# Weight sums by adding transfers, and four more pairs taken back from chunk two's stores

## The chip, the cores and the metric

The kernel runs on one core of a Trainium2 chip. The metric is the device time of one execution in microseconds, the median of the runs. The engines are TensorE (PE in the profile), VectorE (DVE), ScalarE (ACT), GpSimd (POOL) and SyncE (SP, which here issues nearly all transfers).

## What is computed

```python
def _attn_ref(u, v, z):                       # u, v: 4 x 3008 x 256, z: 4 x 3008 x 64
    scores = (1.0 / S) * np.matmul(z, z.transpose(0, 2, 1))
    attn = np.maximum(scores, 0.0) ** 2
    return (u * np.matmul(attn, v)).astype(np.float32)

def _moe_ref(x, w_gate, w_val, w_out):        # x: 12032 x 256, weights 256 x 1536 and 1536 x 256, float64
    gate = 1.0 / (1.0 + np.exp(-(x @ w_gate)))
    return (gate * (x @ w_val) @ w_out).astype(np.float32)
```

The result of the first is the input x of the second. The scores are symmetric: the block of keys i and queries j is the transpose of the block of keys j and queries i. The weights come as 64-bit floats, which the kernel turns into 32-bit ones itself.

## The kernel before, in words

**Tiling.** Each of the four batches has six chunks of 512 queries (c = 0 to 5, the last 448) and twelve pairs of 128 keys (k = 0 to 11). A step g is one (batch, chunk, pair), 288 in all: step 0 to 11 is chunk 0 of batch 0 ("chunk one"), 12 to 23 "chunk two", 24 to 35 "chunk three". Every product is done with operands split in a high part and a rest (ah and al, vh and vl, and so on), so that three matmuls stand for one. In a step TensorE does the scores of a later pair (`pe_scores`, 4 matmuls into the bank sc), the product of this step's pair with v (`pe_pv`, 12, into acc), and from step 24 on the gate and value products of the chunk two before (`pe_gv`, 12, into gv) and its output product (`pe_out`, 6).

**Order.** It is written out by hand (`manual_schedule`): the loop over the steps names, call by call, what each engine's queue gets, and each engine works its queue strictly in order. `post_scores(nxt)` puts Relu and Square on ScalarE (L379, L380, result r), ah on ScalarE or VectorE (L388, L390) and al on VectorE (L391). `gate` puts the sigmoid on ScalarE and a product on VectorE (L549), after which the gv bank is free again. For chunks one and two nxt is two steps ahead, from chunk three on one step.

**Taking blocks back.** `turn` writes r to DRAM turned, block by block, where a later chunk can use the block instead of computing its scores (`kept`, `load_back`). For the first two chunks of batch 0 VectorE has no time to turn. There `stored` pairs (k = 6 to 9) are written as they are (L453), from single buffers that are otherwise weight tiles: chunk two's alternate between the two buffers oh1 and ol1. `arrange` (L420) then copies them within DRAM, 16 issues for each 512x512 block, so that chunks four and five can read them as 32x32 blocks (`late`, `load_back`) and VectorE turns these when they are back (`turn_late`, L483). Steps 12 to 27 issue four such copies each. In chunks four and five `pair` takes the pairs in the order 4, 5, 0 to 3 and then 6 on, so that the late ones do not come first.

**Weights.** Ten jobs (`w_jobs`) turn 64-bit words into 32-bit floats in steps 6 to 35. A job loads raw words (`load_w`, L163, on SP), takes their absolute value on ScalarE, shifts, puts the sign back, and forms the low words' share on VectorE (`low_words`, or piece by piece in `low_by_piece`), adds it (L207, or L217 for a piece), and then splits the sum into a high part (ScalarE, L227) and a rest (VectorE, L230). `plan` says in which step each part is called, before (`w_before`) or after (`w_after`) the step's `post_scores`. The scratch for a piece's share is the single buffer zraw for jobs four to seven.

**SP's queue.** It carries all loads of u, v, z and weights, the stores, the rearranging copies and the loads of blocks. POOL's queue carries no transfer.

Of the kernel before, what the change touches and what calls it, by code (L numbers as in the profile page):

```python
# [8 lines left out]
F32 = mybir.dt.float32  # L9
# [3 lines left out]
U32 = mybir.dt.uint32  # L13
AF = mybir.ActivationFunctionType
ALU = mybir.AluOpType
# [13 lines left out]
def kernel(  # L29
# [19 lines left out]
    nc = tc.nc  # L49
    P = 128  # L50
# [52 lines left out]

    def pair(b, c, k):

        if b == 0 and c in (3, 4) and k < 6:
            return (k + 4) % 6
        if not halved(b, c) or k <= 2 * c:
            return k
        return k + 1 if k < NPAIR - 1 else 2 * c + 1  # L110

    def half(b, c, k):
        return halved(b, c) and k == NPAIR - 1


    def back(b, c, k):
        return kept(b, pair(b, c, k) // 2, c) or late(b, c, k)

    def stored(b, c, k):
        return b == 0 and c < 2 and 6 <= k < 10  # L120

    def late(b, c, k):

        return b == 0 and c in (3, 4) and pair(b, c, k) < 4


    w_tiles = {}
# [37 lines left out]
    class Narrow:  # L165
# [38 lines left out]
                )  # L204

        def add(self):
            nc.vector.tensor_tensor(self.fa, self.fa, self.b.bitcast(F32), op=ALU.add)  # L207

        def low_by_piece(self):
            for r, t in zip(self.part, self.raws):  # L210
# [48 lines left out]
    def prep_z_high(b, s):  # L259
        zt = zt_t[b, s]  # L260
        zP = zp.tile([P, CH], F32R, tag="zP", name="zP")
        zQ = zp.tile([P, CH], F32R, tag="zQ", name="zQ")
        if (b, s) == (0, 1):
            nc.vector.tensor_copy(zP[0:64], zt[0:64])
        else:
            nc.scalar.activation(zP[0:64], zt[0:64], AF.Copy)
        if b > 0:
            nc.scalar.activation(zQ[64:128], zt[64:128], AF.Copy)
        z_t[b, s] = zP, zQ

    def prep_z_low(b, s):
        zt, (zP, zQ) = zt_t.pop((b, s)), z_t[b, s]
        if (b, s) == (0, 0):
            nc.vector.tensor_copy(zQ[64:128], zt[64:128])
        if twice(b, s):
            nc.vector.tensor_tensor(zP[64:128], zt[64:128], f32(zQ[64:128]), op=ALU.subtract)
        nc.vector.tensor_tensor(zQ[0:64], zt[0:64], f32(zP[0:64]), op=ALU.subtract)
        if not twice(b, s):
            nc.sync.dma_start(f32(zQ[64:128]), f32(zP[0:64]))
            nc.sync.dma_start(f32(zP[64:128]), f32(zQ[0:64]))  # L280
# [84 lines left out]
    def post_scores(b, c, k):  # L365
        n = chunk(c)
        sc = sc_t.pop((b, c, k), None)
        if back(b, c, k):
            r = r_t.pop((b, c, k))
        else:  # L370
            if half(b, c, k):
                r = r_t.pop((b, c, k))
            elif stored(b, c, k):
                tag = ("gh4", "gl4", "gh2", "gl2")[k - 6] if c == 0 else ("oh1", "ol1")[k % 2]
                r = one.tile([P, 2, CH], F32, tag=tag, name="r")
            else:
                r = two.tile([P, 2, CH], F32, tag="r", name="r")
            q0 = CH // 2 if half(b, c, k) else 0
            nc.scalar.activation(by_halves(r[:, :, q0:n]), products(sc[:, :, 0 : n - q0]), AF.Relu, scale=scale)  # L379
            nc.scalar.activation(r[:, :, q0:n], r[:, :, q0:n], AF.Square)  # L380
        if early(b, c) and k % 3 == 2:
            ah = one.tile([P, 2, CH], F32R, tag="gh5", name="ah")
            al = one.tile([P, 2, CH], F32R, tag="gl5", name="al")
        else:
            ah = two.tile([P, 2, CH], F32R, tag="ah", name="ah")
            al = two.tile([P, 2, CH], F32R, tag="al", name="al")
        if back(b, c, k) or (b, c) == (0, 2) or (b, c) == (0, 1) and k % 3 or (b, c) == (0, 0) and k in (7, 10):
            nc.scalar.activation(ah[:, :, 0:n], r[:, :, 0:n], AF.Copy)  # L388
        else:
            nc.vector.tensor_copy(ah[:, :, 0:n], r[:, :, 0:n])  # L390
        nc.vector.tensor_tensor(al[:, :, 0:n], r[:, :, 0:n], f32(ah[:, :, 0:n]), op=ALU.subtract)  # L391
        a_t[b, c, k] = ah, al
        r_t[b, c, k] = r
# [21 lines left out]
    def arrange(c, e, n):  # L415

        if (c, e) not in blocks_t:
            blocks_t[c, e] = dram.tile([CH // 32, 32, CH // 32, 32], F32, name=f"blocks_{c}_{e}")
        src = stored_t[c, e][:, 32 * n : 32 * n + 32].rearrange("(G p) q -> p G q", p=32)
        nc.sync.dma_start(blocks_t[c, e][n], src)  # L420
# [39 lines left out]
    def load_back(b, c, k):  # L460
        n = chunk(c)
        if late(b, c, k):
            i = pair(b, c, k)
            t = two.tile([P, 2, CH], F32, tag="osb", name="blocks")
            src = blocks_t[i // 2, c][(i % 2) * 8 : (i % 2) * 8 + 8]
            nc.sync.dma_start(t, src.rearrange("(j a) p G q -> (a p) j (G q)", j=2))
            r_t[b, c, k] = t
            return
        r = two.tile([P, 2, CH], F32, tag="r", name="r")
        if half(b, c, k):  # L470
            nc.sync.dma_start(r[:, :, 0 : CH // 2], half_t[b, c].rearrange("(j p) q -> p j q", p=P))
            r_t[b, c, k] = r
            return
        i = pair(b, c, k)
        src = turned_t[b, i // 2, c][(i % 2) * 256 : (i % 2) * 256 + 256, 0:n]
        nc.sync.dma_start(r[:, :, 0:n], src.rearrange("(j p) q -> p j q", p=P))
        r_t[b, c, k] = r

    def turn_late(b, c, k):
        t = r_t.pop((b, c, k))  # L480
        r = two.tile([P, 2, CH], F32, tag="r", name="r")
        for j in range(2):
            nc.vector.transpose(out=r[:, j], in_=t[:, j])  # L483
        r_t[b, c, k] = r

    def pe_pv(b, c, k):
# [128 lines left out]
    w_load.update({10: [(2, 0)], 11: [(2, 1)]})  # L615
    w_load.update({12 + n: [(3, n)] for n in range(4)})
    w_load.update({17 + n: [(4, n)] for n in range(4)})
    w_load.update({24: [(5, 0), (5, 1)], 25: [(6, n) for n in range(4)], 27: [(7, n) for n in range(4)]})
    w_load.update({26: [(8, 0)], 29: [(9, 0)]})
    w_scratch = [("xh", "xl"), ("oh2", "ol2")] * 2  # L620
    w_scratch += [("oh2", "zraw"), ("ol2", "zraw")] * 2 + [("zraw", "ol2"), ("zraw", "vraw")]
    w_before, w_after, w_raw, w_run = {}, {}, {}, {}

    def plan(i, start):

        def at(when, g, *ops):
            when.setdefault(g, []).extend((i, op) for op in ops)
        at(w_after, start, ("abs",))
        if i < 4:
            at(w_before, start + 1, ("shift",), ("sign", 0))  # L630
            at(w_before, start + 2, ("sign", 1), ("power",))
            at(w_before, start + 3, ("low_words",))
            at(w_before, start + 4, ("add",))
            at(w_before, start + 5, ("high_part",))
            at(w_after, start + 5, ("low_part",))
        elif i < 8:
            at(w_before, start + 1, ("shift",), ("sign", 0), ("sign", 1))
            at(w_before, start + 2, ("low_by_piece",))
            at(w_before, start + 3, ("high_part",))
            at(w_after, start + 3, ("low_part",))  # L640
        else:
            at(w_before, start + 1, ("shift",), ("sign", 0))
            at(w_before if i == 8 else w_after, start + (2 if i == 8 else 1), ("low_by_piece",))
            at(w_after if i == 8 else w_before, start + 2, ("high_part",))
            at(w_after, start + 2, ("low_part",))

    for i, start in enumerate([6, 10, 14, 18, 23, 25, 27, 29, 31, 33]):
# [13 lines left out]
    with tc.manual_schedule():  # L661
# [50 lines left out]
        for g, (b, c, k) in enumerate(steps):  # L712
# [18 lines left out]
            if C == 0:  # L731
                if k + 2 < NPAIR:
                    prep_v_low(0, k + 2)
                if k + 5 < NPAIR:
                    load_v(0, k + 5)
                if k in (2, 3, 5):
                    prep_z_low(0, {2: 3, 3: 4, 5: 5}[k])
                if k in (0, 2, 4):
                    turn_z(0, k // 2 + 3)
            weights(w_before.get(g, ()))  # L740
# [1 line left out]
                post_scores(*nxt)  # L742
            if C == 0 and k + 3 < NPAIR:
                prep_v_high(0, k + 3)
            if C == 0 and k in (1, 2, 4):
                prep_z_high(0, {1: 3, 2: 4, 4: 5}[k])
            for n, s in enumerate(steps[g + 2 : g + 4]):
                if s not in r_t and (back(*s) or half(*s)) and (n == 0 or c == NCH - 1 or late(*s)):
                    load_back(*s)
            if m1:  # L750
                split_h(*m1)
# [7 lines left out]
                prep_v(b, NPAIR - 1)  # L759
            if nxt:  # L760
                turn(*nxt)
            if NPAIR <= g < 28:
                i, n = divmod(g - NPAIR, 4)
                for m in range(4 * n, 4 * n + 4):
                    arrange(i // 2, 3 + i % 2, m)
            if g + 2 < len(steps) and late(*steps[g + 2]):
                turn_late(*steps[g + 2])
            if g >= 3 and not end:
                pe_pv(b, c, k)
            if g in (NPAIR + 2, 2 * NPAIR - 1):  # L770
# [90 lines left out]
```

## Time and profile before

| | us |
|---|---|
| median of 3 runs | 1982.29 (1982.26 to 1982.43) |
| the profiled execution | 1982.5 |
| its span, first to last instruction | 1980.7 |
| TensorE busy | 1971.4 |
| VectorE busy | 1218.6 |
| ScalarE busy | 889.3 |
| GpSimd busy | 0.4 |

The span is the profiled execution without what lies around it, 1.8 us. A matmul in the rows has a busy time that overlaps that of the next one, because matmuls are pipelined; what one costs is read from the distance between starts. A row of a queue (SPq) is the time that the queue needed to issue transfers, not the time of the transfers themselves. Averages over the span hide that the stages differ, so the rows below come from stretches.

### The profile page before, as it was taken

How to read it: one execution, taken by the hardware profiler on the slowest of the kernel's cores; microseconds unless marked ns; L12 is line 12 of the kernel's file. 1: busy time of each engine (PE TensorE's matmuls, PEld its weight loads, DVE VectorE, ACT ScalarE, POOL GpSimd, SP SyncE). 2: the span in 40 equal slices, each digit the busy share in tenths (PEclk: the TensorE clock that was granted, in tenths of full speed). 3: DMA queues.
4: the chain of work that ended last, by engine and by line, in shares of the span. 5: the costliest groups of instructions: out<-in, count | busy, mean ns of one | idle time of the engine just before them, and what ended most of it. 6: DMA issues, size and time to landing. Idle time of an engine off the chain costs nothing.

```text
span 1980.7 us, 24832 instructions
## 1 busy us (share of the span) xinstructions
PE 1971.4 (100%) x9318; PEld 1753.4 (89%) x9318; DVE 1218.6 (62%) x1636; ACT 889.3 (45%) x1209; POOL 0.4 (0%) x5
## 2 busy tenths in 40 slices
PE   9999999999999999999999999999999999999999
PEld 7888888998998888898899888889889988888988
DVE  8998565676565554567666555456766564645443
ACT  8875433554444343355444434345544343433332
POOL 0000000000000000000000000000000000000000
PEclk9999999999999999999999999999999999999999
DMA  8755342535353434263535344345453443424101
GB/s 215 165 134 111 63 115 46 129 68 89 73 108 62 116 57 112 66 156 66 100 60 106 66 101 83 86 97 126 76 97 64 103 75 83 94 75 96 47 11 21
DMA packets 785897, 179.04 MB, mean 90 GB/s; under 512 B 730608, under 2 KB 762608, under 8 KB 785776
## 3 DMA queue, kind: packets, MB, share of 16 engines
q1 hardware_dynamic: 782864, 177.09, 41.7%
q8 instruction: 73, 1.20, 0.3%
q10 hardware_dynamic: 2912, 0.36, 0.1%
q14 instruction: 48, 0.39, 0.1%
HBM read 103.94 MB, written 76.28 MB: 91 GB/s over the span
## 4 chain that ended last, share of the span: by engine, by line
PE 91%; DVE 4%; DMA 1%; SPq 1%; ACT 1%; issue 1%; ACTq 0%; DVEq 0%
PE gv L536 12%; PE gv L538 12%; PE gv L537 12%; PE acc L507 11%; PE acc L502 11%; PE acc L504 10%; PE oacc L582 6%; PE oacc L580 6%; PE oacc L581 6%; PE sc L362 3%; PE sc L361 3%; DVE al L391 1%; DMA turned<-turned 0%; SPq L420 0%; SPq L437 0%
## 5 line engine op out<-in xcount | busy, mean ns | idle before, releaser
L548 ACT ACTIVATE g<-gv 128x512 f32<-128x512 f32 (+1 forms) x288 | 169.4, 588 | 989.3 <-PE gv L538 970.4
L549 DVE TENSOR_TENSOR g<-gv,g 128x512 f32<-128x512 f32 (+1 forms) x288 | 195.1, 677 | 453.0 <-ACT g L548 452.7
L536 PE MATMUL gv<-x,wgh 128*128 128x512 f32 (+1 forms) x1152 | 431.6, 375 | 0.6 <-DVE g L549 0.6
L538 PE MATMUL gv<-x,wgl 128*128 128x512 f32 (+1 forms) x1152 | 431.5, 375 | 0.0
L537 PE MATMUL gv<-x,wgh 128*128 128x512 f32 (+1 forms) x1152 | 431.5, 375 | 0.0
L502 PE MATMUL acc<-ah,vh 128*128 128x512 f32 (+1 forms) x1152 | 428.2, 375 | 1.2 <-ACT ah L388 0.5
L504 PE MATMUL acc<-ah,vl 128*128 128x512 f32 (+1 forms) x1056 | 395.6, 375 | 0.0
L391 DVE TENSOR_TENSOR al<-r,ah 128x1024 fp32r<-128x1024 f32 (+1 forms) x287 | 344.9, 1202 | 28.2 <-ACT ah L388 19.0
L507 PE MATMUL acc<-al,vh 128*128 128x512 f32 (+1 forms) x1152 | 338.5, 375 | 1.0 <-DVE al L391 0.5
L502 PEld LDWEIGHTS acc<-ah,vh 128*128 128x128 f32 x1152 | 217.8, 189 | 29.1 <-ACT ah L388 1.2
L507 PEld LDWEIGHTS acc<-al,vh 128*128 128x128 f32 x1152 | 216.9, 189 | 29.7 <-DVE al L391 4.0
L536 PEld LDWEIGHTS gv<-x,wgh 128*128 128x128 f32 x1152 | 217.7, 189 | 26.9 <-DVE g L549 1.0
L537 PEld LDWEIGHTS gv<-x,wgh 128*128 128x128 f32 x1152 | 217.7, 189 | 25.8
L538 PEld LDWEIGHTS gv<-x,wgl 128*128 128x128 f32 x1152 | 217.7, 189 | 25.8
L390 DVE CAST ah<-r 128x1024 fp32r<-128x1024 f32 (+1 forms) x155 | 106.4, 687 | 201.7 <-ACT r L380 201.7
L504 PEld LDWEIGHTS acc<-ah,vl 128*128 128x128 f32 x1056 | 199.6, 189 | 24.2
L580 PE MATMUL oacc<-hh,woh 128*128 128x512 f32 (+1 forms) x576 | 215.8, 375 | 0.0
L581 PE MATMUL oacc<-hl,woh 128*128 128x512 f32 (+1 forms) x576 | 215.8, 375 | 0.0
L582 PE MATMUL oacc<-hh,wol 128*128 128x512 f32 (+1 forms) x576 | 215.8, 375 | 0.0
L144 DVE TENSOR_TENSOR hl<-g,hh 128x512 fp32r<-128x512 f32 (+1 forms) x288 | 194.1, 674 | 17.5 <-ACT hh L143 17.5
L379 ACT ACTIVATE r<-sc 128x1024 f32<-128x1024 f32 (+2 forms) x177 | 172.2, 973 | 36.3 <-PE sc L362 35.3
L143 ACT ACTIVATE hh<-g 128x512 fp32r<-128x512 f32 (+1 forms) x288 | 175.3, 609 | 24.2 <-DVE g L549 24.2
(80 smaller groups left out, 1607.5 us busy)
## 6 DMA issues: line engine op xcount, KB each, us to landing
turned<-turned SPq DMA_DIRECT2D x780, 64.0 KB, 1.9
r<-turned SPq DMA_DIRECT2D x66, 512.0 KB, 3.9
r<-turned SPq DMA_DIRECT2D x36, 448.0 KB, 3.7
vraw<-in_v_dram SPq DMA_DIRECT2D x44, 256.0 KB, 3.9
uraw<-in_u_dram SPq DMA_DIRECT2D x160, 64.0 KB, 2.4
out_dram<-osb SPq DMA_DIRECT2D x160, 64.0 KB, 1.9
zraw<-in_z_dram SPq DMA_DIRECT2D x70, 64.0 KB, 2.4
half<-turned SPq DMA_DIRECT2D x136, 32.0 KB, 1.6
```

The source lines that it names most:

```text
L144: (eng or nc.vector).tensor_tensor(lo, src, f32(hi), op=ALU.subtract)
L391: nc.vector.tensor_tensor(al[:, :, 0:n], r[:, :, 0:n], f32(ah[:, :, 0:n]), op=ALU.subtract)
L502: nc.tensor.matmul(o, vh[:, j, ds], moving(ah[:, j, 0:n]), start=(k == 0 and j == 0), stop=False)
L504: nc.tensor.matmul(o, vl[:, j, ds], moving(ah[:, j, 0:n]), start=False, stop=False)
L507: nc.tensor.matmul(acc[:, d, 0:n], vh[:, j, ds], moving(al[:, j, 0:n]), start=False, stop=stop)
L536: nc.tensor.matmul(o, wh, moving(xh[:, d, 0:n]), start=(d == 0), stop=False)
L537: nc.tensor.matmul(o, wh, moving(xl[:, d, 0:n]), start=False, stop=False)
L538: nc.tensor.matmul(o, wl, moving(xh[:, d, 0:n]), start=False, stop=(d == NB - 1))
L549: nc.vector.tensor_tensor(gh, product(gv[:, 1, 0:n]), gh, op=ALU.mult)
L580: nc.tensor.matmul(o, wh, moving(hh[:, 0:n]), start=(f == 0), stop=False)
L581: nc.tensor.matmul(o, wh, moving(hl[:, 0:n]), start=False, stop=False)
L582: nc.tensor.matmul(o, wl, moving(hh[:, 0:n]), start=False, stop=(f == NF - 1))
```

## The change

Three things are changed.

- **More blocks are stored and taken back.** Chunks one and two store pairs 4 to 9 instead of 6 to 9. Chunk one's six have a buffer each (gh0, gl0, gh1, gl1, oh0, ol0), chunk two's still alternate between oh1 and ol1. Chunk three takes pairs 0 to 3 from the blocks and computes no scores for them; it uses the same order of pairs as chunks four and five. These blocks are loaded three steps ahead, each as two tiles of 128x512 in the two buffers named vraw. There are 96 rearranging copies instead of 64, five in a step, from step 12 to 31, chunk three's blocks first.
- **Sums by transfers.** For seven weight jobs of 1024 elements per partition VectorE's add is replaced by a transfer that GpSimd issues and that adds its source to what lies in its target: one for each of jobs 0 to 3 (`add`), two for each of jobs 4 to 6 (`low_piece`, one piece a step). High part and rest come half a step to a step later.
- **Moves.** Job 7's loads go from step 27 to 28, the scratch of jobs 4 to 7 changes places, the parts of the last two jobs and the early parts of z move by up to a step.

```diff
     def pair(b, c, k):
-        if b == 0 and c in (3, 4) and k < 6:
+        if b == 0 and c in (2, 3, 4) and k < 6:
             return (k + 4) % 6
...
     def stored(b, c, k):
-        return b == 0 and c < 2 and 6 <= k < 10
+        return b == 0 and c < 2 and 4 <= k < 10
     def late(b, c, k):
-        return b == 0 and c in (3, 4) and pair(b, c, k) < 4
+        return b == 0 and c in (2, 3, 4) and pair(b, c, k) < 4
...
         def add(self):
-            nc.vector.tensor_tensor(self.fa, self.fa, self.b.bitcast(F32), op=ALU.add)
+            nc.gpsimd.dma_start(self.fa, self.b.bitcast(F32), accum_op=ALU.add)
+        def low_piece(self, n):
+            r, t = self.part[n], self.raws[n]
+            b = self.scratch(self.b_tag, 1)
+            fb = b.bitcast(F32)
+            nc.vector.tensor_scalar(b, self.a[:, r], -0x00800000, None, op0=ALU.bitwise_and)
+            nc.vector.scalar_tensor_tensor(
+                fb, t[:, :, 0].bitcast(U32), 2.0**-52, fb, op0=ALU.mult, op1=ALU.mult
+            )
+            nc.gpsimd.dma_start(self.fa[:, r], fb, accum_op=ALU.add)
...
-                tag = ("gh4", "gl4", "gh2", "gl2")[k - 6] if c == 0 else ("oh1", "ol1")[k % 2]
+                tag = ("gh0", "gl0", "gh1", "gl1", "oh0", "ol0")[k - 4] if c == 0 else ("oh1", "ol1")[k % 2]
...
-            t = two.tile([P, 2, CH], F32, tag="osb", name="blocks")
-            nc.sync.dma_start(t, src.rearrange("(j a) p G q -> (a p) j (G q)", j=2))
-            r_t[b, c, k] = t
+            if c > 2:
+                t = two.tile([P, 2, CH], F32, tag="osb", name="blocks")
+                nc.sync.dma_start(t, src.rearrange("(j a) p G q -> (a p) j (G q)", j=2))
+                r_t[b, c, k] = [t[:, 0], t[:, 1]]
+                return
+            r_t[b, c, k] = []
+            for j in range(2):
+                t = two.tile([P, CH], F32, tag="vraw", name="blocks")
+                nc.sync.dma_start(t, src[4 * j : 4 * j + 4].rearrange("a p G q -> (a p) (G q)"))
+                r_t[b, c, k].append(t)
...
-    ... 27: [(7, n) for n in range(4)]})
+    ... 28: [(7, n) for n in range(4)]})
...
         if i < 4:
...
-            at(w_before, start + 3, ("low_words",))
-            at(w_before, start + 4, ("add",))
-            at(w_before, start + 5, ("high_part",))
-            at(w_after, start + 5, ("low_part",))
+            at(w_before, start + 3, ("low_words",), ("add",))
+            at(w_after, start + 5, ("high_part",))
+            at(w_before, start + 6, ("low_part",))
+        elif i < 7:
+            at(w_before, start + 1, ("shift",), ("sign", 0), ("sign", 1))
+            at(w_before, start + 2, ("low_piece", 0))
+            at(w_before, start + 3, ("low_piece", 1))
+            at(w_after, start + 4, ("high_part",), ("low_part",))
...
-            if NPAIR <= g < 28:
-                i, n = divmod(g - NPAIR, 4)
-                for m in range(4 * n, 4 * n + 4):
-                    arrange(i // 2, 3 + i % 2, m)
+            for n in range(5 * (g - NPAIR), min(5 * (g - NPAIR) + 5, 96)):
+                if n >= 0:
+                    arrange(*((0, 2), (1, 2), (0, 3), (0, 4), (1, 3), (1, 4))[n // 16], n % 16)
             if g + 2 < len(steps) and late(*steps[g + 2]):
                 turn_late(*steps[g + 2])
+            if g + 3 < len(steps) and late(*steps[g + 3]) and steps[g + 3][1] == 2:
+                load_back(*steps[g + 3])
```

What stands in SP's queue shows the first part. Before, from the u loads of step 14 to the rearranging copies of step 17 (stored_3 are rows that go to chunk four, blocks_3 the same rearranged; wraw are raw weights):

```order
L326 DMA uraw<-in_u_dram 32x16x32 x8
L163 DMA wraw<-in_moe_w_gate_dram 128x2x256
L420 DMA blocks_3_628<-stored_3_360 512x1x32 x4
L163 DMA wraw<-in_moe_w_val_dram 128x2x256
L453 DMA stored_3_777<-r 128x2x512
L420 DMA blocks_4_779<-stored_4_434 512x1x32 x4
```

And now, from the first store of chunk two (step 14) to that of pair six (step 16):

```order
L463 DMA stored_2_703<-r 128x2x512
L430 DMA blocks_2_631<-stored_2_301 512x1x32 x5
L336 DMA uraw<-in_u_dram 32x16x32 x8
L163 DMA wraw<-in_moe_w_gate_dram 128x2x256
L463 DMA stored_2_703<-r 128x2x512
L430 DMA blocks_2_631<-stored_2_301 512x1x32
L430 DMA blocks_2_754<-stored_2_703 512x1x32 x4
L163 DMA wraw<-in_moe_w_val_dram 128x2x256
L463 DMA stored_3_788<-r 128x2x512
```

Two more stores stand ahead of that of pair six, the u loads now stand between the first two, and the copies of stored_2_703 follow one issue behind its second store.

Still on SP, now from step 20 to the first load of chunk three's blocks in step 23, where before there was no such load:

```order
L430 DMA blocks_3_861<-stored_3_363 512x1x32 x5
L163 DMA wraw<-in_moe_w_val_dram 128x2x256
L430 DMA blocks_3_861<-stored_3_363 512x1x32 x3
L430 DMA blocks_4_971<-stored_4_437 512x1x32 x12
L483 DMA blocks<-blocks_2_631 128x512 x2
```

On VectorE, before, the end of step 24 and step 25 (wo is a weight job's sum, wz its piece's share):

```order
L191 SCALAR_TENSOR_TENSOR wo<-wraw,wo 128x512 x2
L391 TENSOR_TENSOR al<-r,ah 128x1024
L549 TENSOR_TENSOR g<-gv,g 128x512
L213 TENSOR_SCALAR wz<-wo 128x512
L214 SCALAR_TENSOR_TENSOR wz<-wraw,wz 128x512
L217 TENSOR_TENSOR wo<-wo,wz 128x512
```

And now the same place:

```order
L191 SCALAR_TENSOR_TENSOR wo<-wraw,wo 128x512 x2
L401 TENSOR_TENSOR al<-r,ah 128x1024
L500 STREAM_TRANSPOSE r<-blocks 128x512 x2
L566 TENSOR_TENSOR g<-gv,g 128x512
L213 TENSOR_SCALAR wz<-wo 128x512
L214 SCALAR_TENSOR_TENSOR wz<-wraw,wz 128x512
```

The transposes of the loaded blocks stand ahead of the gate product, and the adds are gone.

## Rows read from the trace of the kernel before

**Rows 1.** The page: span, busy times (share, instructions), chain by engine.

```profile
span 1980.7 us, 24832 instructions
...
PE 1971.4 (100%) x9318; PEld 1753.4 (89%) x9318; DVE 1218.6 (62%) x1636; ACT 889.3 (45%) x1209; POOL 0.4 (0%) x5
...
PE 91%; DVE 4%; DMA 1%; SPq 1%; ACT 1%; issue 1%; ACTq 0%; DVEq 0%
```

**Rows 2.** Windows: length, busy PE PEld DVE ACT POOL, clock, DMA share, GB/s.

```profile
80.00:100.00 20.00, 19.89 (x92) 16.86 (x91) 19.23 (x22) 17.70 (x20) 0.00 (x0) 1.00 0.82 182
...
180.00:200.00 20.00, 20.00 (x94) 17.53 (x93) 16.03 (x22) 7.35 (x10) 0.00 (x0) 1.00 0.54 142
```

**Rows 3.** Timeline of TensorE, steps 18 and 25: start, length, instruction, idle before.

```profile
74.18 0.38 PE L361 MATMUL sc<-zP 128*128 128x512 f32 x1
74.40 0.38 PE L362 MATMUL sc<-zQ,zP 128*128 128x512 f32 x1
...
74.83 0.38 PE L362 MATMUL sc<-zQ,zP 128*128 128x512 f32 x1
...
75.55 0.48 PE L502 MATMUL acc<-ah,vh 128*128 128x512 f32 x1 [0.35 <-DVE ah L390]
...
105.86 0.38 PE L536 MATMUL gv<-x,wgh 128*128 128x512 f32 x1
```

**Rows 4.** Timeline of SP's queue, 36 to 110 us, like issues merged.

```profile
47.57 2.62 SPq L420 DMA_DIRECT2D blocks<-stored  x4
...
58.46 4.34 SPq L326 DMA_DIRECT2D uraw<-in_u_dram  x8
...
65.96 0.62 SPq L163 DMA_DIRECT2D wraw<-in_moe_w_val_dram  x1
72.87 0.37 SPq L453 DMA_DIRECT2D stored<-r  x1
...
92.62 10.97 SPq L420 DMA_DIRECT2D blocks<-stored  x16
```

**Rows 5.** Timeline of VectorE, steps 22 to 30.

```profile
94.37 1.22 DVE L207 TENSOR_TENSOR wo<-wo 128x1024 f32<-128x1024 f32 x1
...
99.64 0.69 DVE L184 TENSOR_SCALAR wo<-wo 128x1024 f32<-128x1024 f32 x1 [0.56 <-ACT wo L180]
...
101.10 1.47 DVE L191 SCALAR_TENSOR_TENSOR wo<-wraw,wo 128x512 int32<-128x512 int32 x2
...
103.89 0.68 DVE L549 TENSOR_TENSOR g<-gv,g 128x512 f32<-128x512 f32 x1
...
105.81 0.69 DVE L217 TENSOR_TENSOR wo<-wo,wz 128x512 f32<-128x512 f32 x1
...
139.61 1.30 DVE L433 STREAM_TRANSPOSE turned<-r 128x512 f32<-128x512 f32 x2
```

**Rows 6.** Timeline of ScalarE, steps 11 to 18.

```profile
51.75 1.06 ACT L227 ACTIVATE wgh<-wx 128x1024 fp32r<-128x1024 f32 x1 [0.73 <-DVE wx L207]
...
62.07 1.07 ACT L380 ACTIVATE r<-r 128x1024 f32<-128x1024 f32 x1
...
76.91 1.03 ACT L379 ACTIVATE r<-sc 128x1024 f32<-128x1024 f32 x1 [0.98 <-DVE al L391]
```

**Rows 7.** Transfers, 36 to 100 us: count, size of one, median us to landing.

```profile
stored<-r SPq DMA_DIRECT2D x6, 512.0 KB, 3.5
blocks<-stored SPq DMA_DIRECT2D x48, 64.0 KB, 2.9
wraw<-in_moe_w_gate_dram SPq DMA_DIRECT2D x5, 256.0 KB, 3.5
...
wraw<-in_moe_w_out_dram SPq DMA_DIRECT2D x2, 512.0 KB, 5.0
```

**Rows 8.** Transfers, 0 to 36 us.

```profile
zP<-zQ SPq DMA_DIRECT2D x5, 128.0 KB, 2.5
```

**Rows 9.** Timeline of VectorE, step 9, the first job's low words.

```profile
47.08 1.58 DVE L202 SCALAR_TENSOR_TENSOR wx<-wraw,wx 128x512 f32<-128x512 uint32 x2
```

More of the change, by code (lines that the diff above doesn't have):

```diff
@@ L482, in turn_late @@
         for j in range(2):
-            nc.vector.transpose(out=r[:, j], in_=t[:, j])
+            nc.vector.transpose(out=r[:, j], in_=t[j])
         r_t[b, c, k] = r
@@ L617 @@
     w_load.update({17 + n: [(4, n)] for n in range(4)})
-    w_load.update({24: [(5, 0), (5, 1)], 25: [(6, n) for n in range(4)], 27: [(7, n) for n in range(4)]})
+    w_load.update({24: [(5, 0), (5, 1)], 25: [(6, n) for n in range(4)], 28: [(7, n) for n in range(4)]})
     w_load.update({26: [(8, 0)], 29: [(9, 0)]})
     w_scratch = [("xh", "xl"), ("oh2", "ol2")] * 2
-    w_scratch += [("oh2", "zraw"), ("ol2", "zraw")] * 2 + [("zraw", "ol2"), ("zraw", "vraw")]
+    w_scratch += [("ol2", "zraw"), ("oh2", "zraw")] * 2 + [("zraw", "ol2"), ("zraw", "vraw")]
     w_before, w_after, w_raw, w_run = {}, {}, {}, {}
@@ L642, in plan @@
             at(w_before, start + 1, ("shift",), ("sign", 0))
-            at(w_before if i == 8 else w_after, start + (2 if i == 8 else 1), ("low_by_piece",))
-            at(w_after if i == 8 else w_before, start + 2, ("high_part",))
+            at(w_before if i == 8 else w_after, start + 2, ("low_by_piece",))
+            at(w_after, start + 2, ("high_part",))
             at(w_after, start + 2, ("low_part",))
@@ L735 @@
                     load_v(0, k + 5)
-                if k in (2, 3, 5):
-                    prep_z_low(0, {2: 3, 3: 4, 5: 5}[k])
+                if k in (1, 3, 5):
+                    prep_z_low(0, k // 2 + 3)
                 if k in (0, 2, 4):
@@ L744 @@
                 prep_v_high(0, k + 3)
-            if C == 0 and k in (1, 2, 4):
-                prep_z_high(0, {1: 3, 2: 4, 4: 5}[k])
+            if C == 0 and k in (0, 2, 4):
+                prep_z_high(0, k // 2 + 3)
             for n, s in enumerate(steps[g + 2 : g + 4]):
-                if s not in r_t and (back(*s) or half(*s)) and (n == 0 or c == NCH - 1 or late(*s)):
+                if s not in r_t and (back(*s) or half(*s)) and (n == 0 or c == NCH - 1 or late(*s) and s[1] > 2):
                     load_back(*s)
```

## The prediction, made before the changed kernel had run

> **What bounds the kernel now.** The page first: TensorE has an instruction in flight for 1971.4 of 1980.7 us, and 91% of the chain that ended last is TensorE's [rows 1]. In the windows it is full from 180 us on; before that VectorE is nearly as full, 19.2 us of the 20 from 80 to 100, and TensorE shows gaps [rows 2]. So TensorE's work sets the time, and in the first 180 us anything late on VectorE, ScalarE or a queue reaches it. What is lost there is not got back, since TensorE has no idle time later. Its timeline gives prices: score matmuls of 128x512 start 0.217 us apart (0.65 us for three), and the first matmul of step 18 starts 0.72 us after its forerunner instead, because it waits for ah [rows 3]. By such gaps between starts TensorE stood some 3.3 us in all from 70 to 104 us.
>
> The SP queue comes last, and it decides. SP issues transfers strictly in order. One rearranging issue (L420) costs 10.97 / 16 = 0.69 us of SP's time, a row of eight u loads 4.34 us, a weight load 0.62 us, a store of a pair 0.37 and a gap, say 0.42 us [rows 4]. From 66.6 to 72.87 us SP stands still, waiting for the pair that it is to store; after that it issues without a break until past 103 us. A step of TensorE in chunk two is 16 x 0.217 = 3.5 us, and four rearranging issues (2.8 us), a store and a weight load already fill it.
>
> **TensorE's part.** Four pairs of chunk three lose their scores: 16 matmuls x 0.217 us [rows 3] = 3.5 us, all on the path. Otherwise it does the same matmuls.
>
> **VectorE's and ScalarE's part.** VectorE loses four adds of 1024 elements at 1.22 us and six of 512 at 0.69 us, 9.0 us; it gains eight transposes at 0.65 us, 5.2 us [rows 5]. ScalarE loses four Relu (1.03 us) and four Square (1.07 us), 8.4 us [rows 6]. The first four jobs' adds lie where VectorE is full, so up to the 3.3 us of stalls may go if nothing else is late there. In chunk three, steps 26 and 28 now hold gate 0.7, a piece 1.3, shift and signs 2.9, al 1.2, hl 0.7 and transposes 1.3, some 8 us, against 30 matmuls = 6.5 us; steps 25 and 27 hold 5 and 6.4: no net gain there.
>
> **The adding transfers.** Ten go onto POOL's queue, which holds nothing else. No row shows one. From below: the smallest transfer within SBUF, 128 KB in 2.5 us [rows 8]. From above: 512 KB lands in 5.0 us in this stretch [rows 7], doubled because the sum also reads its target, 10 us. I take 5.0. The first job's low words are ready at 48.7 us [rows 9]; its high part stood on ScalarE at 51.75 us and now stands three instructions of 1.0 to 1.1 us later [rows 6], at 54.9: 6.2 us of cover. Nothing is lost at 5.0, some 4 us at 10, since the next Relu queues behind it on ScalarE and TensorE waits for that. The later jobs have as much or more. In jobs four to six the second piece also waits for the first transfer, because both use the one zraw buffer, with al queued behind it on VectorE; a step, 6.5 us or more, covers it.
>
> **SP's part, the term that I take to decide.** There are 96 rearranging issues for 64, five in a step for four, and they go on to step 31. Chunk two's stored pairs begin at pair four, two steps earlier than at pair six, so SP can no longer run ahead to 66.6 us. It comes to that store at about 57 us (47.57 + 10 x 0.69 + two weight loads) and waits until ScalarE ends the pair's Square at 63.14 us [rows 4, 6]. From there to the first load of chunk three's stored blocks, in step 23, stand six stores, 2.5 us; fifty rearrangings (steps 14 to 23), 50 x 0.69 = 34.5; eight u loads 4.3; six weight loads 3.7; and a new wait, because the blocks of chunk two's first two stored pairs are issued one issue behind the store of the second: it lands 3.5 us after its issue [rows 7], of which 1.1 go on issuing, so 2.4. The sum is 47.4 us. The first load is issued at 110.5 us, the second at 111.0, and its 256 KB land 3.5 us later [rows 7], at 114.5. Its transposes would be due on VectorE at about 103.9, ahead of the gate product of step 25 [rows 5].
>
> Two things hang on that. First, the stored pairs of chunk two alternate between two single buffers (oh1, ol1), so Relu of pair k waits on ScalarE for the store of pair k - 2. By the same prices pair six is stored at 79 us instead of 72.87 and lands at 82 to 83, and Relu of pair eight, at 76.91 us before (released then by al, the other reader of that buffer) [rows 6], starts 5 to 6 us late; TensorE stands for part of that in steps 20 and 21. Second, and later, so that it contains the first: the gate product (L549 before) frees the gv bank, and it now stands behind the transposes. 114.5 + 1.3 (transposes) + 0.7 (gate) = 116.5 us, where TensorE began these matmuls at 105.86 [rows 3, 5]: **10.6 us late**.
>
> The same addition on the kernel before, from 72.87 to 103.59 us (36 rearrangings, four stores, four weight loads), gives 29.0 us where the trace has 30.7 [rows 4], 6% more. With 6% on 47.4 TensorE is 13.4 us late. I take 12. After it, three removed score blocks (2.6 us) are still to be gained; VectorE's steps of 8 us, and the last pair's load, which queues behind eight u loads and nine other issues, can take that back and 2.3 us more. I set the rest at nothing, between -2.6 and +2.3.
>
> One rule speaks against this term. The Trainium skill, "DMA: Bandwidth & Descriptors", section "Issuing engines are not separate DMA queues", says that the issuing sequencer's time "is usually small relative to the DMA itself". By it the sum would be rival A's. The trace does not agree: 0.69 us of issue stands against a landing of 2.9 us [rows 4, 7], and a step holds more of them than fit.
>
> **Sum.** Span 1980.7 + 12 = 1992.7; the profiled execution took 1982.5 us, 1.8 more than its span, so 1994.5; the runs' median is 0.2 below it: **1994.3 us**. The 12 is net of the removed matmuls, being read at a place that TensorE reaches late whatever it saved.
>
> **The rivals.**
> Rival A, faster: SP's lateness never reaches TensorE, because issuing goes faster when more is queued. For it: SP stood idle for 6.3 us before 72.87. Against it: sixteen issues in a row kept 0.69 us. Then 3.5 us of matmuls and none to all of the 3.3 us of stalls go: 1975.5 to 1978.8 us. It holds if the first load is issued by about 98 us. Chance 0.09.
> Rival B, partly hidden: the first load is out at 99 to 107 us, and the delay eats the gain or little more: 1979 to 1989 us. For it: ScalarE is lighter, and the store's wait could be short. Against it: nearly a tenth to a quarter of the 47.4 us would have to go. Chance 0.15, 0.10 of it within 0.2%.
> Rival C, slower by the adds: a transfer that adds takes over 10 us beside DMA engines that are 82% busy [rows 2], so that ScalarE's high part, with Relu behind it, and VectorE's second pieces wait, on top of SP: 1998 to 2012 us. Against it: the first job has 6.2 us of cover, and SP's own wait hides part. Chance 0.12.
> The Trainium skill, "SBUF — State Buffer", section "A bandwidth-pool intuition that's wrong (but worth ruling out)", gives 3.1 us instead of 0.62 us for a GpSimd transfer beside a VectorE copy, an estimate of 2.5 us more for each; no run here shows it. By it rival C would begin at a landing of 3.7 us, and the sum would be 1996 to 1998 us if the first adds land in 5 to 7.5.
> The forecast, 1989 to 2002 us: chance 0.64. Its ends are 10.6 - 2.6 and 13.4 + 2.3 + 4 beyond the median, with the first rounded down.
>
> **How the numbers follow.** A measurement of this kernel tells about 0.2% (4 us) from no change. Faster: rival A, 0.09. Same: the part of rival B from 1978.3 to 1986.3 us, 0.10. Slower: the rest, 0.81. For 8 in 10 the range leaves out rival A, a part of rival B and the top of rival C: 1984 to 2003 us.
>
> **What would show it.** In the profile after: SP without a gap from about 63 us to past 110, at 0.69 us for each rearranging issue; the first loads of chunk three's blocks issued at 110 to 114 us; VectorE idle before the first transposes of blocks, released by that load; TensorE standing in steps 20, 21 and 25, with gv of step 25 at 116 to 120 us; Relu of chunk two's pairs eight and nine released by stores. From step 36 on TensorE should run as before. I am wrong if SP has gaps there, if ScalarE waits for POOL's transfers, or if gv of step 25 starts before 106 us.

## The result, and the profile after

The changed kernel takes 2009.3 us in the median (2008.7 to 2010.2, four runs) against 1982.35 us (1982.26 to 1982.43): ratio 1.0136, 95% interval 1.0123 to 1.0149. It is 27 us slower; the forecast was 12, in a range up to 2003 us.

The page of the changed kernel, span, busy times and chain by engine (before: [rows 1]):

```profile
span 2008.4 us, 24877 instructions
...
PE 1979.5 (99%) x9302; PEld 1755.4 (87%) x9302; DVE 1214.0 (60%) x1634; ACT 880.8 (44%) x1201; POOL 10.1 (1%) x15
...
PE 90%; SPq 3%; DVE 3%; DMA 2%; ACT 1%; issue 1%; ACTq 0%; DVEq 0%
```

TensorE has 16 matmuls less, as planned, and the busy times of the other engines hardly changed. What is new in the chain is SPq, 3% for 1%. The windows tell where (columns as in [rows 2]: length, busy PE PEld DVE ACT POOL, clock, DMA share, GB/s):

```profile
60.00:80.00 20.00, 18.02 (x79) 14.18 (x77) 17.76 (x21) 13.90 (x15) 1.72 (x2) 1.00 0.74 159
80.00:100.00 20.00, 14.29 (x51) 10.36 (x52) 9.89 (x12) 14.68 (x16) 0.00 (x0) 0.91 0.90 197
100.00:120.00 20.00, 15.87 (x63) 12.83 (x62) 12.51 (x14) 11.56 (x13) 0.86 (x1) 0.84 0.83 167
120.00:140.00 20.00, 14.33 (x44) 11.09 (x44) 10.37 (x16) 5.08 (x7) 2.03 (x2) 0.76 0.91 203
140.00:160.00 20.00, 17.49 (x77) 14.58 (x76) 16.60 (x24) 7.83 (x11) 2.03 (x2) 0.97 0.98 212
```

From 80 to 140 us no engine is full any more. VectorE, which was busy for 19.23 us of 80 to 100, now has 9.89: all wait. The lost time stays lost: counted by the first matmul of each step, TensorE is 10.6 us late in step 24, 18.8 at gv of step 25, 23.2 at gv of step 26, and 27.4 from step 37 to the end.

SP's queue in that stretch (start, length, issue, how many merged; before: [rows 4]):

```profile
65.06 0.37 SPq L463 DMA_DIRECT2D stored<-r  x1
65.48 5.04 SPq L430 DMA_DIRECT2D blocks<-stored  x5
...
76.00 7.01 SPq L430 DMA_DIRECT2D blocks<-stored  x5
...
103.69 5.01 SPq L430 DMA_DIRECT2D blocks<-stored  x5
...
109.41 10.15 SPq L430 DMA_DIRECT2D blocks<-stored  x15
119.61 1.09 SPq L483 DMA_DIRECT2D blocks<-blocks  x2
...
125.19 0.90 SPq L163 DMA_DIRECT2D wraw<-in_moe_w_out_dram  x2
```

From the first store to the first load of chunk three's blocks it takes 119.61 - 65.06 = 54.6 us. Fifteen copies in a row keep 0.68 us each. Of the seven rows of five copies ahead of them, three are slower: 5.04 and 5.01 us, 1 us for one, and 7.01, of which 2.9 are the foreseen wait for a store; the other four take 3.7 to 4.3. Behind the loads stand the raw weights of job 5, out at 125.19 instead of 103.71 us.

Who waits for that. ScalarE, then VectorE, then TensorE (in brackets: idle before, and who ended it):

```profile
56.87 1.06 ACT L237 ACTIVATE wgh<-wx 128x1024 fp32r<-128x1024 f32 x1 [2.90 <-DMA wx<-wx]
...
79.63 1.02 ACT L389 ACTIVATE r<-sc 128x1024 f32<-128x1024 f32 x1 [5.91 <-DMA stored<-r]
...
87.90 1.02 ACT L389 ACTIVATE r<-sc 128x1024 f32<-128x1024 f32 x1 [5.07 <-DMA stored<-r]
...
108.90 1.06 ACT L237 ACTIVATE wgh<-wo 128x1024 fp32r<-128x1024 f32 x1 [3.25 <-DMA wo<-wo]
...
131.81 0.90 ACT L180 ACTIVATE wo<-wraw 128x512 f32<-128x512 f32 x1 [6.18 <-DMA wraw<-in_moe_w_out_dram]
```

```profile
122.65 1.37 DVE L500 STREAM_TRANSPOSE r<-blocks 128x512 f32<-128x512 f32 x2 [5.75 <-DMA blocks<-blocks]
...
135.65 0.69 DVE L566 TENSOR_TENSOR g<-gv,g 128x512 f32<-128x512 f32 x1 [6.62 <-ACT g L565]
...
151.09 1.36 DVE L500 STREAM_TRANSPOSE r<-blocks 128x512 f32<-128x512 f32 x2 [3.26 <-DMA blocks<-blocks]
```

```profile
80.71 0.48 PE L371 MATMUL sc<-zP 128*128 128x512 f32 x1 [1.62 <-ACT r L389]
...
88.98 0.48 PE L371 MATMUL sc<-zP 128*128 128x512 f32 x1 [1.55 <-ACT r L389]
...
115.69 0.80 PE L519 MATMUL acc<-ah,vh 128*128 128x512 f32 x1 [4.12 <-ACT ah L398]
...
124.65 0.79 PE L553 MATMUL gv<-x,wgh 128*128 128x512 f32 x1 [3.70 <-DVE g L566]
...
136.40 0.48 PE L553 MATMUL gv<-x,wgh 128*128 128x512 f32 x1 [1.97 <-DVE g L566]
...
153.08 0.48 PE L553 MATMUL gv<-x,wgh 128*128 128x512 f32 x1 [1.78 <-DVE g L566]
```

These are the six stands of over 1.5 us, and they have four causes. At 80.71 and 88.98 Relu of pairs seven and eight waits for the stores of pairs five and six (they share the buffers oh1 and ol1); at 115.69 ScalarE was held by job 3's adding transfer and then 1.15 us by the raw weights that follow; at 124.65 and 153.08 TensorE waits for the transposes of the blocks; at 136.40 for job 5's raw weights, by ScalarE's abs ahead of a Sigmoid. All but the adding transfer's part at 115.69 go back to late issues on SP. By these rows that part adds nothing to the end by itself: TensorE stands again at 124.65, for blocks whose time SP sets.

### The profile page after: what moved, and what is told of

It is laid out like the page before. It is cut to its first block, busy times and chain, and to the rows that moved or that the text cites. A ratio compares the mean times of both kernels' runs of the same rounds, so it can differ in the third digit from the quotient of the medians.

```text
span 2008.4 us, 24877 instructions
## 1 busy us (share of the span) xinstructions
PE 1979.5 (99%) x9302; PEld 1755.4 (87%) x9302; DVE 1214.0 (60%) x1634; ACT 880.8 (44%) x1201; POOL 10.1 (1%) x15
## 4 chain that ended last, share of the span: by engine, by line
PE 90%; SPq 3%; DVE 3%; DMA 2%; ACT 1%; issue 1%; ACTq 0%; DVEq 0%
PE gv L554 12%; PE gv L555 12%; PE gv L553 12%; PE acc L524 11%; PE acc L519 11%; PE acc L521 10%; PE oacc L599 6%; PE oacc L597 6%; PE oacc L598 6%; PE sc L372 3%; PE sc L371 3%; SPq L430 2%; DMA turned<-turned 1%; SPq L447 0%; DMA wraw<-in_moe_w_out_dram 0%
## 5 line engine op out<-in xcount | busy, mean ns | idle before, releaser
L389 ACT ACTIVATE r<-sc 128x1024 f32<-128x1024 f32 (+2 forms) x173 | 168.1, 972 | 45.8 <-PE sc L372 34.9
```

## The experiments

Medians in us, all beside the kernel before (1982.4 to 1982.5); VectorE's adds or adding transfers, with the copies on SP or none:

| | with copies | without copies |
|---|---|---|
| chunk three has its scores, VectorE adds | 1982.5 (before) | 1982.4 (e6) |
| the same, adding transfers | 1989.9 (e2) | 1985.6 (e11) |
| chunk three takes four pairs back, VectorE adds | 2002.8 (e1) | 1985.7 (e5) |
| the same, adding transfers | 2009.3 (after) | 1989.2 (e9) |

Every version but the kernel before and e6 also has the new order of the weight work (the moves, and one piece a step), which was not run by itself.

**The two parts apart (e1, e2).** In e1 both adding lines become VectorE's again; e2 is the changed kernel with the old pairs, copies and scores.

```diff
-            nc.gpsimd.dma_start(self.fa, self.b.bitcast(F32), accum_op=ALU.add)
+            nc.vector.tensor_tensor(self.fa, self.fa, self.b.bitcast(F32), op=ALU.add)
```

> The changed kernel with its ten adding transfers put back onto VectorE as tensor_tensor adds at the same places; everything else as changed. Theory S (SP issues the rearranging copies too slowly, so chunk three's blocks come late): the adds are a minor cause. Job 0's high part no longer waits 2.9 us on ScalarE, and job 3's (4.5 us of TensorE standing in step 25) no longer waits for its transfer, but the loads are issued at 116 to 120 us as before, so 2000 to 2009 us. Theory C (the adding transfers are late and hold ScalarE): most of the 27 us goes, 1980 to 1992 us.

> The other part alone: the changed kernel's adding transfers and small moves, with the stored pairs (six to nine), the 64 copies at four in a step and the scores of chunk three as in the kernel before. Theory S: SP is no later than before, so 1978 to 1986 us; what the transfers take back on ScalarE (2 us in step 11) is about what VectorE gains. Theory C: 1992 to 2005 us, since the high parts wait for the transfers here too.

e1: 2002.8 us, ratio 1.0101 (1.0086 to 1.0116). e2: 1989.9 us, 1.0037 (1.0023 to 1.0051). So the adds cost 6.5 us beside the rest and 7.4 alone (there with the moves), and the pairs taken back, with their copies and the moves, 20.3 us. In e1 SP's store and first load, and TensorE at gv of step 25, then 26:

```profile
63.21 0.37 SPq L463 DMA_DIRECT2D stored<-r  x1
...
113.73 1.09 SPq L483 DMA_DIRECT2D blocks<-blocks  x2
```

```profile
118.78 0.79 PE L553 MATMUL gv<-x,wgh 128*128 128x512 f32 x1 [5.47 <-DVE g L566]
...
129.00 0.48 PE L553 MATMUL gv<-x,wgh 128*128 128x512 f32 x1 [1.26 <-DVE g L566]
```

That is the forecast's ledger without the adds: 50.5 us, and gv of step 25 is 118.78 - 105.86 = 12.9 us late. But gv of step 26 is 15.8 us late (it began at 113.19 before), and the end 20.9.

Neither theory had e2 right: S said no loss, C more. Its largest stand, 3.4 us between starts (113.73 to gv of step 26 at 117.15), hangs on this row of ScalarE in e2:

```profile
112.76 0.88 ACT L180 ACTIVATE wo<-wraw 128x512 f32<-128x512 f32 x1 [5.18 <-DMA wraw<-in_moe_w_out_dram]
```

The raw weights of job 5 again: out 3.5 us later on SP than before (107.23 for 103.71). The adds reach TensorE partly by way of SP's queue.

**Fewer copies in a step (e3, e4, e7).** Three or four for five; e3 takes chunk four's blocks ahead of chunk five's.

```diff
-            for n in range(5 * (g - NPAIR), min(5 * (g - NPAIR) + 5, 96)):
+            for n in range(3 * (g - NPAIR), min(3 * (g - NPAIR) + 3, 96)):
```

> The changed kernel with three rearranging copies in a step instead of five, to step 43 instead of 31, so the same 96 in all; chunk four's blocks of both chunks are made before chunk five's. From the store of pair four (step 14) to the first load of chunk three's blocks (step 23) stand 30 copies instead of 50. Theory S: 20 x 0.69 to 1.0 us less on SP, the first load out by 96 to 105 us instead of 119.6, no waits at stores or transposes worth more than 2 us in all; the 3.5 us of score matmuls show: 1976 to 1984 us. Rival R1 (the loaded blocks hold TensorE by what VectorE and ScalarE must do with them in steps 24 to 29, whenever they come): above 1990 us. Rival C (adding transfers): above 1990 us.

> The changed kernel with four copies in a step, in its own order, to step 35. Forty copies stand between the store of pair four and the first load, ten fewer. Theory S by the forecast's price (0.69 us): 6.9 us earlier, 2000 to 2004 us; by the price seen after the change (up to 1.0 us, and less standing at a lower clock): 10 us earlier or more, 1990 to 1999 us. Rivals R1 and C: within 4 us of the changed kernel, 2005 to 2013 us.

> The run with three copies in a step (1998.4 us), with one more change: in each step the loads of chunk three's blocks are issued behind the step's weight loads instead of ahead of them. In that run SP stood 3.1 us before the load for step 27, because its buffers (vraw) wait for the transposes of the pair before, and the raw weights of job 5 stood behind it; ScalarE then waited 4.4 + 1.4 us for them ahead of a gate's Sigmoid. Theory H (that wait at the head of the queue costs TensorE what it stood at that place): 1.5 to 4 us less, 1994 to 1997 us. Rival R1 (VectorE's load in steps 24 to 29 sets it): within 1.5 us of 1998.4.

e3: 1998.4 us, ratio 1.0079 (1.0064 to 1.0094). e4: 2005.6, 1.0116 (1.0101 to 1.0131). e7, which issues chunk three's blocks behind the step's weight loads: 1998.35, 1.0080 (1.0065 to 1.0095). The pace counts (2009.3, 2005.6, 1998.4 at five, four, three), but far less than S said, and by these three alone the rivals stood better: first loads left at 119.6, 111.8 and 104.1 us. A part of what the slower pace gains is given back: in e3, e4 and e7 copies are still in the queue near chunk four, ScalarE there waits 5.4 to 6.4 us for turned blocks (`r<-turned`), and TensorE falls back by another 4.3, 5.0 and 3.6 us from step 34 on, where e1 loses 0.2. e7 moved a stand and took nothing away: the wait at the head of the queue isn't what is left.

**No copies (e5, e6).** The late pairs are gathered straight from the stored rows, eight transfers of 64 KB each; in e5, with VectorE's adds, chunk three's go into oh1 and ol1, behind the weight loads of steps 22 to 25.

```diff
-            src = blocks_t[i // 2, c][(i % 2) * 8 : (i % 2) * 8 + 8]
+            src = stored_t[i // 2, c]
...
+            for j in range(2):
+                for a in range(4):
+                    n = 8 * (i % 2) + 4 * j + a
+                    nc.sync.dma_start(
+                        t[32 * a : 32 * a + 32, j].rearrange("p (G q) -> p G q", q=32),
+                        src[:, 32 * n : 32 * n + 32].rearrange("(G p) q -> p G q", p=32),
+                    )
```

> The changed kernel with VectorE's adds and without any rearranging copy: each late pair (of chunks three, four and five) is gathered in eight transfers of 64 KB straight from the stored rows, for chunk three into oh1 and ol1 at the ends of steps 22 to 25, so that SP and the DMA engines are free of 96 copies in steps 12 to 31. Against the run with VectorE's adds alone (2002.8 us). Theory S/D (the copies, by SP's time or the DMA engines', are what makes everything behind them on SP late): no store, weight load or block load late, 1976 to 1986 us. Rival R1 (VectorE has too much to do in steps 24 to 29 once eight transposes are added, whatever the queue does): two or three stands of 2 us there remain, 1986 to 1994 us.

> The kernel before without its 64 copies: the late pairs of chunks four and five are gathered in eight transfers of 64 KB straight from the stored rows; chunk three keeps its scores. Theory S/D: the kernel before was already at the edge on SP, so what it stands from 70 to 104 us (some 3 us) partly goes, 1978 to 1982 us, unless the eight transfers in a row in steps 36 to 53 hold others up. Rival: the copies cost the kernel before nothing, 1982 to 1984 us.

e5: 1985.7 us, ratio 1.0015 (1.0006 to 1.0024), 17.1 us less than e1: **the copies are the loss** (e14 below has the same buffers and nearly the same place of the loads, but the copies, and gains nothing). e6: 1982.4 us, 1.0000 (0.9990 to 1.0009): in the kernel before the same kind of copies cost nothing. The 3.5 us of removed matmuls don't show in e5, and its windows point to VectorE:

```profile
100.00:120.00 20.00, 18.62 (x85) 15.54 (x85) 19.69 (x30) 8.54 (x12) 0.00 (x0) 1.00 0.58 122
```

VectorE is busy for 19.69 of 20 us; clock 1.00, DMA share 0.58. At gv of step 26 e5 is 1.3 us ahead of the kernel before (111.93 for 113.19), having skipped two pairs' scores; its next steps take 8.0, 7.0, 9.1, 7.3 and 8.9 us, where the kernel before has 7.3 in each, and at step 32 it is 2.6 behind.

**By which way (e8, e13, e14).** e8 is e1 with the copies issued by POOL (`nc.gpsimd.dma_start`). e13 and e14 load chunk three's blocks whole into oh1 and ol1, behind the weight loads, with the copies on POOL and on SP; all with VectorE's adds.

```diff
-                t = two.tile([P, CH], F32, tag="vraw", name="blocks")
+                t = one.tile([P, 2, CH], F32, tag=("oh1", "ol1")[k % 2], name="blocks")
```

> The run with VectorE's adds (2002.8 us) with its 96 copies issued from POOL's queue instead of SP's; same bytes, same order among themselves. Theory S (SP's time for an issue is the limit): stores, weight loads and block loads are no longer behind copies, 1984 to 1994 us. Theory D (the DMA engines, nearly all busy with rows of 128 bytes, are the limit, and SP's 0.69 us is their pace pushed back): 1998 us or more, and SP's other issues get longer.

> The run with POOL's copies (1991.3 us), with chunk three's blocks loaded whole into oh1 and ol1 (free in these steps) instead of in halves into vraw, and behind each step's weight loads. In that run SP stood from about 90 to 104.6 us before the load for step 27, job 5's raw weights left at 105.6, and TensorE stood 5.25 us. Theory H (the wait at the head of SP's queue is what was left there above 1985.7): 1985 to 1988 us. Theory D (the DMA engines are slower beside the copies, whoever issues them): 1989 to 1992 us.

> The run with VectorE's adds and five copies in a step on SP (2002.8 us), with the same own buffers and order of loads. Theory S (SP's time for issues makes the first loads late, whatever waits at its head): the first load leaves SP at about 115 us still, 1997 to 2003 us. Theory H (the wait at the head of the queue is the larger part of 17 us): 1988 to 1995 us.

e8: 1991.3 us, ratio 1.0044 (1.0029 to 1.0059), in S's range. e13: 1989.85, 1.0037 (1.0023 to 1.0051). e14: 2005.8, 1.0118 (1.0102 to 1.0133). e13 and e14 differ by the copies' queue alone, and by 16 us. SP's queue in e13, then in e14:

```profile
86.61 0.37 SPq L479 DMA_DIRECT2D blocks<-blocks  x1
96.30 0.88 SPq L163 DMA_DIRECT2D wraw<-in_moe_w_out_dram  x2
```

```profile
103.95 9.92 SPq L430 DMA_DIRECT2D blocks<-stored  x15
113.91 0.62 SPq L479 DMA_DIRECT2D blocks<-blocks  x1
...
118.03 1.06 SPq L163 DMA_DIRECT2D wraw<-in_moe_w_out_dram  x2
```

And the windows from 100 to 120 us, e13 and e14:

```profile
100.00:120.00 20.00, 18.31 (x84) 15.25 (x83) 17.55 (x25) 7.32 (x10) 18.44 (x29) 1.00 0.95 265
```

```profile
100.00:120.00 20.00, 10.80 (x47) 8.52 (x47) 11.39 (x14) 8.19 (x10) 0.00 (x0) 0.90 0.77 143
```

With POOL's queue the DMA engines do more (share 0.95 for 0.77), and TensorE hardly stands. So the engines weren't what cost the 16 us (theory D). But e13's time fell into D's range, and D isn't refuted for what is left: beside POOL's copies the four loads of blocks landed 7.2 to 9.1 us after their issue, in e14 4.1 to 5.9. Of the 4 us between e13 and e5, 3.1 are one stand at 120 us, for the third load, which I had put behind step 25's u loads and which landed 7.6 us after its issue; no run tells the place from the landing. Own buffers didn't help e14 (theory H), which ended above S's range. What costs is that SP's other transfers queue behind the copies. What sets 0.65 to 0.70 us for a copy stays open: in e8 POOL issued eighteen in 12.61 us, the same pace.

**The adds without copies (e9, e10, e11, e15).** e9 is the changed kernel with e5's gathers; e10 the same with jobs 0 to 3 added by VectorE, so that only the six pieces are transfers; e11 the adds alone, e15 the pieces alone, both with chunk three's scores.

> The changed kernel, adding transfers included, with the gathers of the run with direct loads in place of its 96 copies. Against that run (1985.7 us), where VectorE does the adds. Theory S (the adding transfers cost what they did, 6.5 to 7.4 us, by lengthening SP's issues and landings while the copies filled the queue): without copies they cost little, and they take 0.7 us from each of the steps of VectorE in which TensorE still stands 1.6 to 1.7 us: 1978 to 1985 us. Rival C' (an adding transfer is late by itself, wherever it runs): 1988 to 1994 us.

> As the run with direct loads and adding transfers, but jobs 0 to 3 are added by VectorE; only the six pieces of jobs 4 to 6 are added by transfers. In chunk two the high part on ScalarE then waits for VectorE instead of a transfer of 512 KB (6.5 us). Theory S: within 2 us of the run with all adds as transfers, 1978 to 1985 us, better if job 0's and job 3's waits for the transfer are what is left. Rival C': 1986 to 1992 us.

> The adding transfers alone (chunk three with all its scores, stored pairs from six), without copies: chunks four and five gather in eight transfers as in the kernel before without copies (1982.4 us). Theory S: the 7.4 us that the adds cost beside 64 copies goes: 1980 to 1984 us. Rival C': 1987 to 1991 us.

> No copies, chunk three with all its scores, and of the ten adds only the six pieces of jobs 4 to 6 by transfers. Theory: jobs 0 to 3's transfers are what costs 3.1 us in the run with the adds alone and no copies (1985.6 us, its stands lie between 58 and 99 us), and the pieces' take 0.7 us from VectorE where the kernel before still stands 1.4 us (step 24) : 1979 to 1982 us. Rival (a transfer takes back what it gives): 1982 to 1984 us.

e9: 1989.15 us, ratio 1.0032 (1.0020 to 1.0044). e10: 1984.15, 1.0008 (0.9999 to 1.0017). e11: 1985.6, 1.0014 (1.0005 to 1.0024). e15: 1983.4, 1.0004 (0.9995 to 1.0013). The adds of jobs 0 to 3 cost 5.0 us in e9 against e10 (2.1 in e11 against e15) with no copy near. That goes against my theory, which allowed 2 us between e9 and e10: e9 is where rival C' had it, e11 between the two. ScalarE in e11:

```profile
57.08 1.06 ACT L237 ACTIVATE wgh<-wx 128x1024 fp32r<-128x1024 f32 x1 [3.35 <-DMA wx<-wx]
```

The high part waits as in the changed kernel, so the transfer is late by itself. The pieces save 1.5 us beside the late pairs (e10 against e5) and nothing that can be measured without them: e15 is 1.0 us above e6, as its rival had it.

**VectorE's share (e12, e16).** e12 is e5 with ScalarE copying chunk three's blocks, untransposed, so that four pairs of that chunk are multiplied untransposed; e16 is e10 with the clamp of each job from job 4 on moved to POOL.

> The run with direct loads and VectorE's adds (1985.7 us), with the eight transposes of chunk three's loaded pairs left out: ScalarE, which is busy less than half of that stretch, copies the blocks as they are. So four pairs of chunk three are multiplied untransposed; all else is computed as it should be. Theory R1 (VectorE's 1.3 us in each of steps 24 to 27 is what is left above the kernel before, and hides the 3.5 us of removed score matmuls): three stands of 1.6 to 1.7 us shrink, 1979 to 1983 us. Rival (what is left comes from elsewhere): 1984 to 1987 us.

> The run with direct loads and the pieces' transfers (1984.2 us), with one of VectorE's instructions of each weight job from job 4 on, the clamp of 1024 elements (0.69 us), put on POOL. Theory R1 (VectorE sets the pace of steps 24 to 31): the stands of 1.1 to 1.6 us there shrink by up to 0.7 each, 1980.5 to 1983.5 us. Rival (POOL is slower at it than VectorE has time, or holds VectorE up at SBUF): 1985 to 1995 us.

e12: 1984.2 us, ratio 1.0008 (0.9999 to 1.0017), at the rival's lower end: the transposes are 1.5 us of it, not all. Stands of 1.3 to 1.7 us at 124, 130 and 146 us stay, with VectorE at the later weight jobs. The last two lie in steps 28 and 30, which take 9.1 and 8.9 us from gv to gv in e5 as in e12, and 7.3 before, though no loaded block is turned in them. Before, both pieces of a job stood in the odd steps from 25 on, and shift and signs of the next job in the even ones; now the second piece stands in the even steps too. No run puts the old order back.

e16: 1998.3 us, 1.0077 (1.0064 to 1.0090), slower than e10 by 14 and above its rival's range too. VectorE in e16:

```profile
118.16 0.69 DVE L186 TENSOR_SCALAR wo<-wo 128x1024 int32<-128x1024 int32 x1 [4.88 <-POOL wo L185]
```

Four such waits, one of 1.5 and three of 4.9 us, reach TensorE as stands of 1.5 and 3.3 to 5.3 us; so VectorE's chain is the path here, and a clamp that takes POOL 3.6 to 4.0 us can't be lent to it. No version was faster than the kernel before by more than a measurement tells.

## Why the prediction was wrong

**What bounds the kernel, and the way of part (a): right.** SP issues without a gap from 65 us, blocks leave late, VectorE stands ahead of their transposes, the gate product ahead of gv of step 25, and TensorE doesn't get the time back: each has its row above. Relu of pairs seven and eight waits for stores, a pair sooner than I wrote.

**"The sum is 47.4 us" and "I take 12": right for the pairs and copies alone.** e1 has 50.5 us, which is 6.6% more (I allowed 6%), and 12.9 us at gv of step 25. The changed kernel has 54.6 us, begun 1.9 us later, and 18.8: the difference is the adds'. The later begin is job 0's high part, behind which ScalarE works without a gap up to the Square of pair four. The longer issues stand beside the transfers: worked from SP's single rows, the 35 copies issued within 5.5 us after an adding transfer took 0.94 us in the mean, the other 61 0.71 (medians 0.67 and 0.63; a few took 1.3 to 3.7). In e1 the mean of all 96 is 0.73. Of the 50 copies ahead of the first load, 14 are of the first kind; they took 4.2 us more in all than the same 14 in e1, the other 36 0.2 us less.

**"Nothing is lost at 5.0": wrong, 6.5 us.** Job 0's transfer left at 48.79 us and held the high part, for which ScalarE was free at 53.97, until 56.87: cover 5.2 us, not 6.2, and 8.1 us to use, not 5.0. Job 3's held it 3.25 us, so "the later jobs have as much or more" failed too. That ScalarE waits for POOL's transfers was one of my own signs of being wrong. What I left out is the way by SP: at gv of step 25 the changed kernel is 5.9 us behind e1, as much as the later begin and the longer issues make. Rival C named the place but not the size: it asked for transfers of over 10 us, and its 1998 to 2012 us holds the time by another sum. Even alone and without copies the adds cost 3.1 us (e11); beside copies, where they also lengthen SP's issues, 7.4 (e2).

**"I set the rest at nothing, between -2.6 and +2.3": wrong, 8 us in e1.** I followed one user of SP's lateness, the blocks. Job 5's raw weights stand behind them on the same queue; ScalarE's abs waits for them ahead of the next Sigmoid, and gv of step 26 loses 2.9 us more in e1, 4.4 in the changed kernel. Its sign was in the rows before: they left SP at 103.71 us, and ScalarE already waited 1.2 us for them.

```profile
103.71 1.07 SPq L163 DMA_DIRECT2D wraw<-in_moe_w_out_dram  x2
```

```profile
108.02 0.88 ACT L180 ACTIVATE wo<-wraw 128x512 f32<-128x512 f32 x1 [1.20 <-DMA wraw<-in_moe_w_out_dram]
```

The remaining 5 us go from step 26 to step 32, where e5, without copies, loses 3.9 us against the kernel before and has VectorE all but full; I had written "no net gain there" and bounded the loss of the rest at 2.3 us.

**Why the 3.5 us never show.** A pair taken back saves TensorE 4 x 0.217 = 0.87 us and costs VectorE 1.3 us, where VectorE is all but full. Without copies the four pairs and the moves still lose 3.3 us (e5 against e6). The transposes are 1.5 of it (e12); how much of the rest is the new order of the weight pieces (steps 28 and 30 above) stays open.

**The clock.** Not foreseen. Before, the windows shown have 1.00 [rows 2]; in the changed kernel it is 0.91, 0.84 and 0.76 where TensorE was busy for only 14 to 16 of 20 us, that is, part of the time it had 1.2 GHz instead of 2.4. Of what each matmul started later than 0.217 us after its forerunner, from 20 us to the end, 25.5 us lie in delays of over 0.26 us and 10.8 in smaller ones; before, 4.2 and 1.3. So some 9.5 us of the loss are matmuls at a lower pace, on top of the stands that they follow; e5, which stands little, has 2.5 in the smaller ones.

**The rule weighed against SP's term.** The Trainium skill, "DMA: Bandwidth & Descriptors", section "Issuing engines are not separate DMA queues", says that the issuing sequencer's time is usually small beside the transfer. For one copy of e14 that is 0.63 us of SP beside a landing of 3.2 (medians); for 96 in one queue it is no guide, since e13 against e14 puts 16 us on which sequencer issues them.

The 27 us, from the table: adds and pairs taken back, with the moves, without copies 6.7 (1989.15 - 1982.4), the copies on top of them 20.

## What to carry to other kernels

Price a queue by all its users: list each transfer that stands behind the added issues, with the engine that waits for it, and take the one that already waits a little as the first to cost something. A price read from a quiet row is a lower bound for a busy one; when a sum decides, take the price from the place where other queues write too. Before trading one engine's work for another's, put the two prices side by side in the steps where they fall: 0.87 us off TensorE for 1.3 us onto VectorE gained nothing here, where both were all but full.

## What the runs showed that I had not expected

An adding transfer within SBUF is no cheaper than a store to memory: in the changed kernel 512 KB landed in 8.1 and 5.0 us (wx) and in 4.6 and 5.6 (wo), where a store of 512 KB took 4.0 in the median; it keeps POOL 0.86 to 1.17 us to issue. In long rows a copy of 64 KB kept POOL 0.65 to 0.71 us (e8, e13), as it did SP. A clamp of 128x1024 took 3.6 to 4.0 us on POOL where VectorE has 0.69.
